# Layer norm as a multiply-add with a precomputed offset, the next chunk's attention norm begun three slots earlier, V projections with a nearer due time

## The chip, the cores and the metric

The kernel runs on one core of a Trainium2 chip. The metric is the device time of one execution in microseconds (us). Engine names follow the profile: PE is the matrix engine (PEld its weight loads), DVE the vector engine, ACT the scalar engine, POOL is GpSimd, and SP is the engine whose queue issues most DMAs here. DMAs are written SPq or POOLq by the queue that issues them. L12 is line 12 of the kernel before; the changed kernel's lines are numbered three higher between L176 and L474 (L182 before is L185 after, L215 is L218, L232 is L235, L339 is L342, L367 is L370).

## The reference, cut to what matters

Two identical layers, each a sliding-window attention (32 heads of 16, window 256) and a ReLU feed-forward (512 to 1792 to 512), each with a layer norm ahead and a residual behind. The sequence is 2048 tokens of width 512.

```python
def _layernorm(x, axis=-1, eps=1e-5):
    m = jnp.mean(x, axis=axis, keepdims=True)
    v = jnp.var(x, axis=axis, keepdims=True)
    return (x - m) / jnp.sqrt(v + eps)
...
    x = x + _A_ref(_layernorm(x, axis=-1), A_wqkv, A_wo)   # qkv, masked softmax, wo
    x = x + _B_ref(_layernorm(x, axis=-1), B_w1, B_w2)     # relu(x @ w1) @ w2
    x = x + _A_ref(_layernorm(x, axis=-1), A_wqkv, A_wo)
    x = x + _B_ref(_layernorm(x, axis=-1), B_w1, B_w2)
```

## The kernel before, in words

The sequence is cut into chunks of 512 tokens, four per layer, so there are eight **steps** k = 0 to 7 (layer k // 4, chunk k mod 4). Every step has 20 **slots**: four head groups t (u counts them through the program) times five groups g of key blocks. Slot 47, say, is step 2, slot +7. All activations stay in SBUF: x_sb holds the residual rows in fp32.

In one slot the program emits, in this order on PE: the score matmuls into Sps (S below), half of the slot's dense budget, the matmuls of probabilities and V into acc (A below, for the head group of five slots ago), and the other half of the budget. Beside them ACT computes the exponentials (Pb<-Sps, L251, two per slot), and the masks are set by DVE (L271) for groups 0, 3 and 4 and by POOL (L257, affine select, six per slot) for groups 1 and 2. The whole order of the matmuls is fixed: in_order (L85) ties each to the one before. The order on the other engines is chosen by the tile scheduler.

The dense budget (L524 to L543) is about nine 512-column matmuls per slot, taken by run_tasks (L447) from a list of tasks with an earliest slot and a due slot; the ready task with the nearest due slot goes first, and equal ones in the order in which they were added. The tasks are: Q and K projections of head group t (add_qk, 8 matmuls, due at slot 20k + 5t - 2), V projections of 128 tokens (add_v, 4 matmuls each), the output projection of half a chunk (plan_wo, 8 matmuls, O below, due at once), and the feed-forward of a chunk (plan_ffn, 56 + 56 matmuls, due late: 20(k+1) + 32). force (L458) runs overdue tasks at once, but only those whose due slot is 3 modulo 5. All dense matmuls share two PSUM buffers, ps_d, which DVE empties (L199, L215, L232, L339, L354, L367).

The layer norm (ln_rows, L178) of a chunk takes, for each 128 tokens, the statistics on DVE (L171, L172, L174), the power -1/2 on POOL (L175, result rstd), the subtraction and multiplication on POOL (L182, result xnA for attention or xnB for the feed-forward, two buffers each), and a transposing DMA from SP's queue into xnT or xn2T (L184). xnT and xn2T have one buffer each. So the transposes for the next chunk wait until the last Q, K or V matmul of the present chunk has read xnT. Tokens 2 and 3 of four (in blocks of 128) wait on POOL besides, until blocks 0 and 1 have been transposed out of the two xnA buffers.

For step k + 1, begin (L491) emits this norm in slot 20k + 5, and its Q, K and V tasks may start from slot 20k + 8. The feed-forward norm of step k is emitted behind its two output projections, around slots +4 and +6 of the next step. The first chunk's norm is written out by itself (L470 to L480) with PE transposes instead of DMAs: L474 runs on DVE for even blocks and on POOL for odd ones.

Of the kernel before, what the change touches and what calls it, by code (L numbers as in the profile page):

```python
# [9 lines left out]
FP32 = mybir.dt.float32  # L10
# [39 lines left out]
def kernel(  # L50
# [10 lines left out]
    nc = tc.nc  # L61
    S = A_x.shape[1]
# [5 lines left out]
    KC = D // P  # L68
# [9 lines left out]
    small = ctx.enter_context(tc.tile_pool(name="small", bufs=2))  # L78
# [18 lines left out]
    def mmt(o, i, idn):  # L97
        inst = nc.tensor.transpose(o, i, idn)
        if chained[0]:
            in_order(inst)  # L100
# [66 lines left out]
    def ln_stats(c, sfx, j0, j1, src=None):  # L167
        mv = small.tile([P, 4, 2], FP32, name="mv" + sfx)
        for j in range(j0, j1):
            st = small.tile([P, 6], FP32, name="st" + sfx)  # L170
            nc.vector.bn_stats(out=st[:], in_=x_sb[:, 4 * c + j, :] if src is None else src[:, j, :])  # L171
            nc.vector.bn_aggr(out=mv[:, j, :], in_=st[:])  # L172
        rstd = small.tile([P, 4], FP32, name="rstd" + sfx)
        nc.vector.tensor_scalar_add(rstd[:, j0:j1], mv[:, j0:j1, 1], 1e-5)  # L174
        nc.gpsimd.tensor_tensor(out=rstd[:, j0:j1], in0=rstd[:, j0:j1], in1=mhalf[:, j0:j1], op=ALU.pow)  # L175
        return rstd, mv  # L176

    def ln_rows(c, xnT, sfx, j0, j1):  # L178
        rstd, mv = ln_stats(c, sfx, j0, j1)
        for j in range(j0, j1):  # L180
            xn = work.tile([P, D], BF16, name="xn" + sfx, bufs=2)
            nc.gpsimd.tensor_scalar(out=xn[:], in0=x_sb[:, 4 * c + j, :], scalar1=mv[:, j, 0:1],  # L182
                                    scalar2=rstd[:, j:j + 1], op0=ALU.subtract, op1=ALU.mult)
            nc.sync.dma_start_transpose(out=xnT[:, :, j * P:(j + 1) * P],  # L184
                                        in_=xn[:].rearrange("p (kc d) -> p kc d", kc=KC))  # L185

# [4 lines left out]
    def q_items(xnT, Qt, t):  # L191
        ps = []

        def one(kc):
            if kc == 0:
                ps.append(ps_d.tile([P, 512], FP32, name="ps_d"))
            mm(ps[0][:], wqkv[:, kc, t * P:(t + 1) * P], xnT[:, kc, :], kc == 0, kc == KC - 1)
            if kc == KC - 1:
                nc.vector.tensor_copy(Qt[:], ps[0][:])  # L199
        return [lambda kc=kc: one(kc) for kc in range(KC)]  # L200

    def k_items(layer, c, xnT, t):
        ps = []
        s0 = slot(layer, 8 * c)
        runs = [(0, 8)] if s0 + 8 <= NSLOT else [(0, NSLOT - s0), (NSLOT - s0, 8)]

        def one(kc):
            if kc == 0:
                ps.append(ps_d.tile([P, 512], FP32, name="ps_d"))
            mm(ps[0][:], wqkv[:, kc, D + t * P:D + (t + 1) * P], xnT[:, kc, :], kc == 0, kc == KC - 1)  # L210
            if kc == KC - 1:
                for a, b in runs:
                    sa = (s0 + a) % NSLOT
                    for e in range(2):
                        nc.vector.tensor_scalar(out=KBD[:, t, sa:sa + b - a, 64 * e:64 * e + 64],  # L215
                                                in0=ps[0][:, 64 * a:64 * b].rearrange("p (s k) -> p s k", k=64),
                                                scalar1=par[:, e:e + 1], scalar2=None, op0=ALU.mult)
        return [lambda kc=kc: one(kc) for kc in range(KC)]  # L218
# [155 lines left out]
    SPS = 20  # L374
# [13 lines left out]
    def start_qkv(k):  # L388
        xnTs[k] = work.tile([P, KC, 512], BF16, name="xnT", tag="xnT", bufs=1)

    def add_qk(k, t, earliest):
        layer, c = divmod(k, NCH)
        holder = {}

        def make():
            Q[k, t] = work.tile([P, 512], BF16, name="Qt", bufs=6)
            return q_items(xnTs[k], Q[k, t], t) + k_items(layer, c, xnTs[k], t)

        def first():
# [68 lines left out]

    start_qkv(0)
    for h in range(2):  # L470
        rstd0, mv0 = ln_stats(0, "S%d" % h, 2 * h, 2 * h + 2, src=xst0)
        for j in range(2 * h, 2 * h + 2):
            xn = work.tile([P, D], BF16, name="xnA", bufs=2)
            (nc.gpsimd if j % 2 else nc.vector).tensor_scalar(  # L474
                out=xn[:], in0=xst0[:, j, :], scalar1=mv0[:, j, 0:1], scalar2=rstd0[:, j:j + 1],
                op0=ALU.subtract, op1=ALU.mult)
# [3 lines left out]
            (nc.scalar.copy if j % 2 else nc.vector.tensor_copy)(xnTs[0][:, :, j * P:(j + 1) * P], tp[:])  # L480
# [19 lines left out]
    def total_left():  # L500
        return sum(len(x[3]) for x in tasks)
# [169 lines left out]
```

## Time and profile before

| what | value |
|---|---|
| time, median of 2 runs | 679.56 us (679.39 to 679.73) |
| profiled execution, own time | 677.07 us |
| its span, first to last instruction | 675.3 us |
| PE busy in the span | 501.4 us (74%) |
| DVE, POOL, ACT busy | 392.9, 326.8, 295.2 us |
| mean granted PE clock | 0.878 |
| PE waiting for xnT | 71.8 us in 6 waits |

The span is 1.8 us shorter than the same execution's time, which has the launch and the end around it. A row of the timeline gives a start, a length, the engine, the line, output and inputs, a count where instructions are merged, and in square brackets how long the engine had stood idle and what ended that. A busy PE is not PE at its peak, so the idle rows and the granted clock tell more than the 74%.

### The profile page before, as it was taken

The page shows a single profiled execution, that of the slowest core. Times are in us where ns is not written, and L with a number is a line of the kernel's source. Part 1 is how long each engine was busy: PE and PEld are TensorE (multiplying, and loading weights), DVE is VectorE, ACT ScalarE, POOL GpSimd, SP SyncE. Part 2 cuts the span into 40 slices and gives each one's busy share as a digit, 9 for nine tenths or more (in the row PEclk, how much of TensorE's full clock was granted, in tenths as well). Part 3 has the DMA queues.
Part 4 walks back from the last instruction along what each step waited for, and adds up shares of the span by engine and source line. Part 5 has one row for each costly group of instructions (what it writes and reads, how often), then busy time and mean ns, then how long its engine had stood idle before and what let it go on. Part 6 is the DMA issues. An engine that isn't in the chain of part 4 may idle for free.

```text
span 675.3 us, 13941 instructions
## 1 busy us (share of the span) xinstructions
PE 501.4 (74%) x5741; PEld 235.2 (35%) x5741; DVE 392.9 (58%) x914; ACT 295.2 (44%) x323; POOL 326.8 (48%) x505
## 2 busy tenths in 40 slices
PE   5658668899189980899648984589937996798194
PEld 2223333444034440344313441234413443344042
DVE  6868447867367580775728673385628647454161
ACT  1353765566235660465414562256534666262000
POOL 9854757224923459233582255523575346332501
PEclk8879659999779995899969996799979999798698
DMA  9410111002200022001210012000230012003102
GB/s 295 172 32 1 34 32 33 2 1 33 55 9 2 2 48 47 1 2 10 54 34 1 2 24 55 16 3 9 49 55 17 2 33 48 17 9 56 32 1 37
DMA packets 59001, 23.02 MB, mean 34 GB/s; under 512 B 50480, under 2 KB 58416, under 8 KB 58928
## 3 DMA queue, kind: packets, MB, share of 16 engines
q1 hardware_dynamic: 56624, 19.94, 13.2%
q0 software_dynamic: 2304, 2.10, 2.1%
q8 instruction: 47, 0.77, 0.5%
q14 instruction: 26, 0.21, 0.1%
HBM read 7.86 MB, written 2.10 MB: 15 GB/s over the span
## 4 chain that ended last, share of the span: by engine, by line
PE 40%; DVE 22%; POOL 18%; issue 11%; DMA 5%; ACT 3%; SPq 0%; POOLq 0%; ACTq 0%
PE ps_d L93 30%; DVE V L232 8%; POOL xnB L182 7%; PE acc L93 6%; PE Sps L93 4%; DVE KBD L215 4%; POOL xnA L182 4%; POOL Pb L257 3%; DVE Pb L271 3%; ACT Pb L251 3%; DMA xnT<-xnA 3%; DMA OT<-O 2%; POOL rstdB L175 1%; DVE stB L171 1%; DVE x_sb L339 1%
## 5 line engine op out<-in xcount | busy, mean ns | idle before, releaser
L251 ACT ACTIVATE Pb<-Sps 128x1024 bf16<-128x1024 f32 (+2 forms) x320 | 292.7, 968 | 301.4 <-PE Sps L93 186.4
L257 POOL TENSOR_SCALAR_AFFINE_SELECT Pb<-Pb 64x256 bf16<-64x256 bf16 x368 | 153.3, 417 | 208.7 <-ACT Pb L251 190.3
L93 PE MATMUL ps_d<-xnT,wqkv 128*128 128x512 bf16 x256 | 79.5, 434 | 82.8 <-DMA xnT<-xnA 71.8
L93 PE MATMUL ps_d<-xn2T,w 128*128 128x512 bf16 x448 | 117.9, 387 | 26.2 <-DMA xn2T<-xnB 21.3
L93 PE MATMUL ps_d<-w,hT 128*128 128x512 bf16 x448 | 112.5, 379 | 0.0
L93 PEld LDWEIGHTS <-Pb 128*128 128x128 bf16 x2880 | 95.8, 97 | 44.7 <-issue 11.7
L354 DVE TENSOR_SCALAR hT<-ps_d 128x512 bf16<-128x512 f32 x112 | 76.3, 687 | 54.5 <-PE ps_d L93 54.4
L93 PE MATMUL acc<-V,Pb 128*128 128x34 bf16 x2880 | 98.6, 179 | 2.4 <-POOL Pb L257 2.1
L93 PE MATMUL Sps<-Qt,KBD 32*128 32x320 bf16 (+4 forms) x1408 | 71.4, 267 | 18.5 <-ACT Pb L251 16.8
L271 DVE TENSOR_TENSOR Pb<-Pb,tri 128x512 bf16<-128x512 bf16 (+1 forms) x152 | 60.1, 425 | 35.4 <-ACT Pb L251 34.6
L182 POOL TENSOR_SCALAR xnB<-x_sb,mvB,rstdB 128x512 bf16<-128x512 f32 x32 | 67.0, 2097 | 1.8 <-DMA xn2T<-xnB 0.2
L199 DVE CAST Qt<-ps_d 128x512 bf16<-128x512 f32 x32 | 22.0, 687 | 75.2 <-PE ps_d L93 75.0
L93 PEld LDWEIGHTS <-wqkv 128*128 128x128 bf16 x256 | 22.9, 106 | 117.8 <-issue 87.5
L93 PEld LDWEIGHTS <-w 128*128 128x128 bf16 x448 | 37.2, 98 | 72.0 <-issue 38.3
L182 POOL TENSOR_SCALAR xnA<-x_sb,mvA,rstdA 128x512 bf16<-128x512 f32 x28 | 57.8, 2071 | 8.4 <-DMA xnT<-xnA 7.7
L232 DVE CAST V<-ps_d 64x256 bf16<-64x256 f32 x128 | 54.0, 422 | 2.1
L93 PEld LDWEIGHTS <-KBD 32*128 32x128 bf16 x1408 | 25.7, 93 | 83.4 <-issue 79.7
L215 DVE TENSOR_SCALAR KBD<-ps_d,par 128x512 bf16<-128x512 f32 (+1 forms) x80 | 47.2, 634 | 11.6 <-PE ps_d L93 11.6
L93 PEld LDWEIGHTS <-hT 128*128 128x128 bf16 x448 | 37.4, 97 | 41.6 <-issue 6.9
L93 PE MATMUL ps_d<-wo,OT 128*128 128x512 bf16 x128 | 38.8, 434 | 13.0 <-DMA OT<-O 9.3
L93 PE MATMUL ps_d<-wqkv,xnT 128*128 128x512 bf16 x128 | 37.8, 382 | 13.4 <-DVE V L232 6.6
L367 DVE TENSOR_TENSOR x_sb<-ps_d,x_sb 128x512 f32<-128x512 f32 x32 | 22.0, 689 | 36.9 <-PE ps_d L93 34.9
(59 smaller groups left out, 228.9 us busy)
## 6 DMA issues: line engine op xcount, KB each, us to landing
w<-in_B_w_dram SPq DMA_DIRECT2D x2, 1792.0 KB, 13.7
out_dram<-x_sb POOLq DMA_DIRECT2D x16, 128.0 KB, 2.8
wqkv<-in_A_wqkv_dram SPq DMA_DIRECT2D x3, 512.0 KB, 6.6
xst<-in_A_x_dram SPq DMA_DIRECT2D x3, 512.0 KB, 9.3
xst<-in_A_x_dram SPq DMA_DIRECT2D x2, 256.0 KB, 3.2
wo<-in_A_wo_dram SPq DMA_DIRECT2D x1, 512.0 KB, 8.8
OT<-O SPq DMA_TRANSPOSE x32, 2.5
xn2T<-xnB SPq DMA_TRANSPOSE x32, 2.4
```

The costliest lines, as they stand in the source:

```text
L93: inst = nc.tensor.matmul(o, lhsT=lhsT, rhs=rhs, start=start, stop=stop)
L171: nc.vector.bn_stats(out=st[:], in_=x_sb[:, 4 * c + j, :] if src is None else src[:, j, :])
L175: nc.gpsimd.tensor_tensor(out=rstd[:, j0:j1], in0=rstd[:, j0:j1], in1=mhalf[:, j0:j1], op=ALU.pow)
L182: nc.gpsimd.tensor_scalar(out=xn[:], in0=x_sb[:, 4 * c + j, :], scalar1=mv[:, j, 0:1], scalar2=rstd[:, j:j + 1], op0=ALU.subtract, op1=ALU ...
L199: nc.vector.tensor_copy(Qt[:], ps[0][:])
L215: nc.vector.tensor_scalar(out=KBD[:, t, sa:sa + b - a, 64 * e:64 * e + 64], in0=ps[0][:, 64 * a:64 * b].rearrange("p (s k) -> p s k", k=64 ...
L232: nc.vector.tensor_copy(V2[64 * e:64 * e + 64, sl, :, 17 * e:17 * e + 16], v4[64 * half:64 * half + 64, :, e, :])
L251: nc.scalar.activation(pv4[:, 2 * rp:2 * rp + 2, 64 + a:64 + z], Sps[rp][:, :, a:z], ACT.Exp, scale=0.25)
L257: nc.gpsimd.affine_select(out=v, in_=v, pattern=[[0, 4], [-1 if far else 1, 64]], compare_op=ALU.is_gt if far else ALU.is_ge, fill=0.0, ba ...
L271: nc.vector.tensor_tensor(out=v, in0=v, in1=m, op=ALU.min)
L354: nc.vector.tensor_relu(hT[:, f, n0:n1], ps[0][:, n0:n1])
L367: nc.vector.tensor_tensor(out=x_sb[:, b, :], in0=ps[0][:], in1=x_sb[:, b, :], op=ALU.add)
```

## The change

Four edits. ln_stats computes one more small vector on DVE, nb = -mean times rstd, behind the power on POOL, and returns it instead of the means. ln_rows on POOL then does x times rstd plus nb instead of (x minus mean) times rstd. The first chunk's norm does the same as an ACT activation (Identity, with scale rstd and bias nb) for all four blocks. begin moves from slot 20k + 5 to 20k + 2, the earliest slot of the Q and K tasks from 20k + 8 to 20k + 5, that of the V tasks to 20k + 7, and the due slot of the V tasks from 20k + 3 to 20k - 1 (which is 4 modulo 5, so that force no longer takes them).

```diff
@@ ln_stats, ln_rows
-        return rstd, mv
+        nb = small.tile([P, 4], FP32, name="nb" + sfx)
+        nc.vector.scalar_tensor_tensor(out=nb[:, j0:j1], in0=mv[:, j0:j1, 0], scalar=-1.0, in1=rstd[:, j0:j1],
+                                       op0=ALU.mult, op1=ALU.mult)
+        return rstd, nb
...
-            nc.gpsimd.tensor_scalar(out=xn[:], in0=x_sb[:, 4 * c + j, :], scalar1=mv[:, j, 0:1],
-                                    scalar2=rstd[:, j:j + 1], op0=ALU.subtract, op1=ALU.mult)
+            nc.gpsimd.tensor_scalar(out=xn[:], in0=x_sb[:, 4 * c + j, :], scalar1=rstd[:, j:j + 1],
+                                    scalar2=nb[:, j:j + 1], op0=ALU.mult, op1=ALU.add)
@@ add_v
-        add_task(earliest, SPS * k + 3, [first] + [lambda: holder["i"].pop(0)() for _ in range(KC - 1)])
+        add_task(earliest, SPS * k - 1, [first] + [lambda: holder["i"].pop(0)() for _ in range(KC - 1)])
@@ first chunk
-            (nc.gpsimd if j % 2 else nc.vector).tensor_scalar(
-                out=xn[:], in0=xst0[:, j, :], scalar1=mv0[:, j, 0:1], scalar2=rstd0[:, j:j + 1],
-                op0=ALU.subtract, op1=ALU.mult)
+            nc.scalar.activation(xn[:], xst0[:, j, :], ACT.Identity, bias=nb0[:, j:j + 1], scale=rstd0[:, j:j + 1])
@@ the steps
-        at_slot(SPS * k + 5, begin)
+        at_slot(SPS * k + 2, begin)
...
-            add_qk(k + 1, t, SPS * k + 8)
+            add_qk(k + 1, t, SPS * k + 5)
...
-            add_v(k + 1, j, SPS * k + 8)
+            add_v(k + 1, j, SPS * k + 7)
```

On PE the change moves the dense matmuls between slots. Step 2, counted from the two programs (Q for a Q or K projection, F1 and F2 for the feed-forward, bold for the chunk after):

| slot | before | after |
|---|---|---|
| 42 | S8 F2x4 A19 F2x5 | S8 F2x4 A19 F2x2 Qx3 |
| 43 | S12 F2x4 A19 F2x5 | S12 Qx4 A19 Qx1 |
| 44 | S12 Ox4 A19 Ox4 F2x1 | S12 Ox4 A19 Ox4 |
| 45 | S8 F2x5 A20 F2x2 Qx3 | S8 **Qx5** A20 **Qx5** |
| 46 | S8 Ox4 A19 Ox4 Qx1 | S8 Ox4 A19 Ox4 **Qx1** |
| 47 | S8 Qx4 A19 | S8 **Vx4** A19 **Vx5** |
| 48 | S12 **Qx4** A19 **Qx5** | S12 **Vx4** A19 **Vx3 Qx2** |
| 49 | S12 **Qx4** A19 **Qx3 Vx2** | S12 **Qx4** A19 **Qx5** |
| 50 | S8 **Vx4** A20 **Vx5** | S8 **Qx2** F1x2 A20 F1x5 |
| 51, 52 | **Vx5 Qx8** F1x5 | F1x18 |

The last matmul that reads the present chunk's xnT, and the first that needs the next one's, are neighbours before (slots 47 and 48), and have slot 44 between them after (slots 43 and 45). Steps 3, 4 and 6 read alike, with the last reader just ahead of the A run of slot +3 in steps 4 and 6. In step 5 it stands in slot +4, ahead of the A run there. In step 0 the change puts the first Q of chunk 1 directly behind chunk 0's last, in slots 4 and 5; before, slots 5 to 7 lay between.

POOL's queue in step 2 (rstdA and xnA belong to the attention norm, xnB and rstdB to the feed-forward's, Pb_132 is slots 46 and 47), before:

```order
L175 TENSOR_TENSOR rstdB<-rstdB,mhalf 128x2
L182 TENSOR_SCALAR xnB<-x_sb,mvB,rstdB 128x512 x2
L175 TENSOR_TENSOR rstdA<-rstdA,mhalf 128x4
L257 AFFINE_SELECT Pb_132<-Pb_132 64x4x64 x6
L175 TENSOR_TENSOR rstdB<-rstdB,mhalf 128x2
L257 AFFINE_SELECT Pb_132<-Pb_132 64x4x64
L182 TENSOR_SCALAR xnB<-x_sb,mvB,rstdB 128x512 x2
L257 AFFINE_SELECT Pb_132<-Pb_132 64x4x64 x2
L182 TENSOR_SCALAR xnA<-x_sb,mvA,rstdA 128x512 x2
L257 AFFINE_SELECT Pb_132<-Pb_132 64x4x64 x3
L182 TENSOR_SCALAR xnA<-x_sb,mvA,rstdA 128x512 x2
```

and in the changed kernel:

```order
L175 TENSOR_TENSOR rstdA<-rstdA,mhalf 128x4
L185 TENSOR_SCALAR xnA<-x_sb,rstdA,nbA 128x512 x4
L175 TENSOR_TENSOR rstdB<-rstdB,mhalf 128x2
L185 TENSOR_SCALAR xnB<-x_sb,rstdB,nbB 128x512 x2
L260 AFFINE_SELECT Pb_132<-Pb_132 64x4x64 x6
L175 TENSOR_TENSOR rstdB<-rstdB,mhalf 128x2
L185 TENSOR_SCALAR xnB<-x_sb,rstdB,nbB 128x512 x2
L260 AFFINE_SELECT Pb_132<-Pb_132 64x4x64 x6
```

The four xnA rows (blocks 2 and 3 of the next chunk, then blocks 0 and 1 of the one behind it) have moved from behind both feed-forward norms to ahead of both.

DVE's queue of the changed kernel in the same place, from the cast behind the first Q matmuls of slot 45 (KBD, V and Qt empty ps_d, L342 is the residual add of the output projection in slot 46):

```order
L174 TENSOR_SCALAR rstdB<-mvB 128x2
L202 CAST Qt<-ps_d 128x512
L177 SCALAR_TENSOR_TENSOR nbB<-mvB,rstdB 128x2
L218 TENSOR_SCALAR KBD<-ps_d,par 128x8x64 x2
L342 TENSOR_TENSOR x_sb<-ps_d,x_sb 128x512
L171 BN_STATS stB<-x_sb 128x6
L172 BN_AGGR mvB<-stB 128x2
L342 TENSOR_TENSOR x_sb<-ps_d,x_sb 128x512
L171 BN_STATS stB<-x_sb 128x6
L172 BN_AGGR mvB<-stB 128x2
L174 TENSOR_SCALAR rstdB<-mvB 128x2
L177 SCALAR_TENSOR_TENSOR nbB<-mvB,rstdB 128x2
```

Each nbB is new and stands in DVE's queue behind a power that POOL computes; the four V casts of slot 47 follow directly.

More of the change, by code (lines that the diff above doesn't have):

```diff
@@ L175, in ln_stats @@
         nc.gpsimd.tensor_tensor(out=rstd[:, j0:j1], in0=rstd[:, j0:j1], in1=mhalf[:, j0:j1], op=ALU.pow)
-        return rstd, mv
+        nb = small.tile([P, 4], FP32, name="nb" + sfx)
+        nc.vector.scalar_tensor_tensor(out=nb[:, j0:j1], in0=mv[:, j0:j1, 0], scalar=-1.0, in1=rstd[:, j0:j1],
+                                       op0=ALU.mult, op1=ALU.mult)
+        return rstd, nb
     def ln_rows(c, xnT, sfx, j0, j1):
-        rstd, mv = ln_stats(c, sfx, j0, j1)
+        rstd, nb = ln_stats(c, sfx, j0, j1)
         for j in range(j0, j1):
             xn = work.tile([P, D], BF16, name="xn" + sfx, bufs=2)
-            nc.gpsimd.tensor_scalar(out=xn[:], in0=x_sb[:, 4 * c + j, :], scalar1=mv[:, j, 0:1],
-                                    scalar2=rstd[:, j:j + 1], op0=ALU.subtract, op1=ALU.mult)
+            nc.gpsimd.tensor_scalar(out=xn[:], in0=x_sb[:, 4 * c + j, :], scalar1=rstd[:, j:j + 1],
+                                    scalar2=nb[:, j:j + 1], op0=ALU.mult, op1=ALU.add)
             nc.sync.dma_start_transpose(out=xnT[:, :, j * P:(j + 1) * P],
@@ L470 @@
     for h in range(2):
-        rstd0, mv0 = ln_stats(0, "S%d" % h, 2 * h, 2 * h + 2, src=xst0)
+        rstd0, nb0 = ln_stats(0, "S%d" % h, 2 * h, 2 * h + 2, src=xst0)
         for j in range(2 * h, 2 * h + 2):
             xn = work.tile([P, D], BF16, name="xnA", bufs=2)
-            (nc.gpsimd if j % 2 else nc.vector).tensor_scalar(
-                out=xn[:], in0=xst0[:, j, :], scalar1=mv0[:, j, 0:1], scalar2=rstd0[:, j:j + 1],
-                op0=ALU.subtract, op1=ALU.mult)
+            nc.scalar.activation(xn[:], xst0[:, j, :], ACT.Identity, bias=nb0[:, j:j + 1], scale=rstd0[:, j:j + 1])
             tp = ps_d.tile([P, KC, P], BF16, name="tp", tag="ps_d")
```

## The prediction

> **What bounds the kernel now.** I read the totals first, then PE's waits in order of size, then the timeline around each long one.
>
> ```profile
> span 675.3 us, 13941 instructions
> PE ps_d L93 <- DMA xnT<-xnA: 71.8, 6, 17.3
> PE ps_d L93 <- DMA xn2T<-xnB: 21.3, 2, 14.7
> PE ps_d L93 <- DMA OT<-O: 9.3, 4, 4.9
> ```
>
> The columns are total us, times, longest. PE follows a fixed order, so a matmul that waits holds everything behind it. The six waits for xnT, the normalised and transposed input of the next chunk, are the largest loss. They are these rows (the wait stands in brackets), with one wait for OT in the same step as the fifth:
>
> ```profile
> 49.96 1.87 PE L93 MATMUL ps_d<-xnT,wqkv 128*128 128x512 bf16 x4 [4.64 <-DMA xnT<-xnA]
> 187.07 1.87 PE L93 MATMUL ps_d<-xnT,wqkv 128*128 128x512 bf16 x4 [15.18 <-DMA xnT<-xnA]
> 269.13 1.87 PE L93 MATMUL ps_d<-xnT,wqkv 128*128 128x512 bf16 x4 [17.25 <-DMA xnT<-xnA]
> 346.57 1.86 PE L93 MATMUL ps_d<-xnT,wqkv 128*128 128x512 bf16 x4 [12.99 <-DMA xnT<-xnA]
> 408.79 1.89 PE L93 MATMUL ps_d<-wo,OT 128*128 128x512 bf16 x4 [4.91 <-DMA OT<-O]
> 429.16 1.87 PE L93 MATMUL ps_d<-xnT,wqkv 128*128 128x512 bf16 x4 [12.36 <-DMA xnT<-xnA]
> 503.32 1.87 PE L93 MATMUL ps_d<-xnT,wqkv 128*128 128x512 bf16 x4 [9.39 <-DMA xnT<-xnA]
> ```
>
> Together 76.7 us, one row or pair for each of steps 0 and 2 to 6. Why 15 us in step 2:
>
> ```profile
> 169.63 1.02 PE L93 MATMUL ps_d<-xnT,wqkv 128*128 128x512 bf16 x4 [0.24 <-DVE x_sb L339]
> 171.51 2.57 SPq L184 DMA_TRANSPOSE xnT<-xnA  x2
> 175.29 4.13 POOL L182 TENSOR_SCALAR xnB<-x_sb,mvB,rstdB 128x512 bf16<-128x512 f32 x2
> 180.38 4.12 POOL L182 TENSOR_SCALAR xnA<-x_sb,mvA,rstdA 128x512 bf16<-128x512 f32 x2
> 182.47 3.25 SPq L184 DMA_TRANSPOSE xnT<-xnA  x2
> ```
>
> The last reader of the old xnT ends at 170.65. Only then do the first two transposes go out, and only behind them can POOL write blocks 2 and 3, since xnA has two buffers. But POOL takes xnB first, so 16.4 us pass from the last reader to the next Q matmul, and PE has one run of work to put in between. The wait is a serial chain behind the release of xnT, not lack of POOL time as such.
>
> **The chain without POOL's detour.** Step 0 has it nearly bare:
>
> ```profile
> 38.88 1.04 PE L93 MATMUL ps_d<-xnT,wqkv 128*128 128x512 bf16 x4 [0.82 <-DVE KBD L215]
> L184 SPq DMA_TRANSPOSE xnT<-xnA x4: 1189/1190/1312, 40.1 to 47.4; - x4
> DMA to landing us min/median/max: 2.4/2.5/3.1
> 42.87 2.08 POOL xnA L182
> 47.41 2.41 DMA xnT<-xnA
> ```
>
> Released at 39.92, issued at 40.1 (0.2), landed after 2.5, two POOL rows of 2.07, the last transpose 2.4, and 0.15 to the matmul: 9.4 us (10.0 measured there, with a power in between).
>
> **Term 1, the waits: -35.3 us.** In the changed POOL queue the xnA rows stand ahead of xnB, so I take 9.4 for the chain. Between release and first use now lies slot 44's work, whose size is seen before:
>
> ```profile
> 158.61 0.40 PE L93 MATMUL Sps<-Qt,KBD 32*128 32x64 bf16 x12
> 158.94 1.04 PE L93 MATMUL ps_d<-wo,OT 128*128 128x512 bf16 x4
> 159.82 0.63 PE L93 MATMUL acc<-V,Pb 128*128 128x34 bf16 x19
> 161.62 0.38 PE L93 MATMUL ps_d<-w,hT 128*128 128x512 bf16 x1
> 161.93 0.40 PE L93 MATMUL Sps<-Qt,KBD 32*128 32x256 bf16 x8
> ```
>
> A slot start to the next is 3.32; less one feed-forward matmul (0.38), plus the next S (0.40) and 0.3 for ACT's pace: 3.6 us of cover. Steps 2 and 3 then wait 9.4 - 3.6 = 5.8 each. Steps 4 and 6 have an A run more (0.6): 5.2 each. In step 5 the release stands in slot +4, with 0.9 of cover, and one xnB row precedes xnA on POOL (1.8 more): 10.3. In step 0 nothing but an S lies between (0.3): 9.1, worse than its 4.64 now. Sum 41.4 against 76.7. The transposes for OT's second half now queue on SP behind xnT's four; they go out when the last xnT one does, and their matmuls come a slot after the first Q, so they are covered. The wait never falls below 5 us, so PE's cold restart stays: four matmuls in 1.87 instead of 1.04.
>
> **Term 2, the start: -2.5 us.**
>
> ```profile
> 9.93 2.08 POOL L474 TENSOR_SCALAR xnA<-xst,mvS,rstdS 128x512 bf16<-128x512 bf16 x1
> 11.69 0.11 DVE L155 MEMSET V<- 64x64 bf16 x1 [0.26 <-issue]
> 13.85 0.59 ACT L480 COPY xnT<-tp 128x512 bf16<-128x512 bf16 x1 [11.79 <-PE tp L98]
> 16.53 2.10 POOL L474 TENSOR_SCALAR xnA<-xst,mvS,rstdS 128x512 bf16<-128x512 bf16 x1
> 19.96 3.06 PE L93 MATMUL ps_d<-xnT,wqkv 128*128 128x512 bf16 x8 [0.67 <-ACT xnT L480]
> ```
>
> nbS stands in DVE's queue behind ten memsets, the last at 11.69, so ACT begins at 12.0. Four activations and two copies at 0.6 to 0.7 each, with the PE transposes between, end near 16.7 instead of 19.9: 3 us, of which I give back 0.5, since nbA of chunk 1 makes DVE wait for POOL's casts ahead of the first Qt. The Trainium skill (ScalarE: Activation LUTs, What ACT_TABLE_LOAD costs) has an activation with two pointer operands at about 0.8 us for this size, an estimate from its formula, against 0.59 for the copy row; that would take 0.5 us more from this term.
>
> **Term 3, moved slots: -2.5 us.** Three slots with nothing but S and A leave the stretch of steps 0 and 1 that goes at ACT's pace:
>
> ```profile
> 70.40:107.80 37.40, 25.34 (x363) 13.15 (x361) 16.66 (x45) 25.23 (x29) 25.42 (x36) 0.59 0.18 36
> L251 ACT ACTIVATE Pb<-Sps 128x1024 bf16<-128x1024 f32 x272 | 263.6, 1021 | 268.1 <-PE Sps L93 153.2 <-issue 89.6 <-ACT Pb L251 23.2
> ```
>
> That is 14.5 slots in 37.4 us with 16 cold O matmuls in it: 2.4 us a slot, near two exponentials of 1.02. The three are done later at PE's own 1.2 a slot, which saves 3.6; step 7 gets two such slots more than before (its Q work is done earlier) and pays about 1.1 net.
>
> **Term 4, new holds: +12 us.** This is what the change adds. nb on DVE waits for rstd from POOL, and POOL is deep in xnA and xnB by then.
>
> ```profile
> L182 POOL TENSOR_SCALAR xnB<-x_sb,mvB,rstdB 128x512 bf16<-128x512 f32 x32 | 67.0, 2097 | 1.8 <-DMA xn2T<-xnB 0.2 <-POOL rstdB L175 0.2
> L175 POOL TENSOR_TENSOR rstdB<-rstdB,mhalf 128x2 f32<-128x2 f32 x16 | 11.7, 729 | 60.0 <-DVE rstdB L174 59.7
> L257 POOL TENSOR_SCALAR_AFFINE_SELECT Pb<-Pb 64x256 bf16<-64x256 bf16 x368 | 153.3, 417 | 208.7 <-ACT Pb L251 190.3
> ```
>
> With R the release: POOL's xnA rows end at R + 12 (the last two wait for a landing). The first nbB stands behind a Qt cast that itself comes at R + 11.7 and so costs half a microsecond. POOL's first xnB pair ends at R + 17 (power 0.7, pair 4.2), six affine selects (2.5, and they wait for slot 46's exponentials) near R + 20, the second power at R + 21; DVE reaches its nbB near R + 19.7 and is held 1.3, with V casts behind it and PE behind those. The projection stretch also gets O's two adds and statistics, which DVE used to do before the wait. How much that costs is seen from two stretches with the same 40 projection matmuls:
>
> ```profile
> 187.07:205.30 18.23, 16.15 (x172) 6.92 (x173) 13.29 (x29) 7.43 (x8) 5.55 (x8) 0.84 0.01 1
> 107.80:124.60 16.80, 13.73 (x176) 6.24 (x173) 14.69 (x35) 9.38 (x10) 9.70 (x15) 1.00 0.09 18
> ```
>
> The first follows a wait (clock 0.84), the second has the statistics in it (DVE x35) and no wait ahead, and is no longer. So 1.5 us per step for the holds, 9 in six steps. xn2T is next: its second half is ready about 13 us after slot 46's O, by then PE has done some 13 us of projections and wants it in slot 50, two slots sooner than now. I give 0.5 a step, 3 in all; without this cover a step would lose up to 4.
>
> **Term 5, POOL's multiply-add: 0.** No row shows it. The nearest:
>
> ```profile
> L182 POOL TENSOR_SCALAR xnA<-x_sb,mvA,rstdA 128x512 bf16<-128x512 f32 x28 | 57.8, 2071 | 8.4 <-DMA xnT<-xnA 7.7
> L484 POOL CAST x_sb<-xst 128x512 f32<-128x512 bf16 x12 | 6.8, 608 | 0.0
> ```
>
> Same operand shapes, two operations, two pointers: I take 2.07. From below it could be a cast's 0.61, from above the sum of the two, 2.68. Two of these rows lie in each of six chains, two in step 7's wait for xn2T (21.3 less 14.7: 6.6) and some two in the tail's 14.7: sixteen rows on the path, so -23 us to +10 us. The Trainium skill (GPSIMD Engine Reference, 3.1 Elementwise) puts a one-input body at 1.03 to 1.8 cycles an element; that is 0.44 to 0.77 us here, an estimate, and by it the sum would be some 20 to 26 us lower. The subtract-multiply row, at 2.07, does not agree with it.
>
> **Sum.** -35.3 - 2.5 - 2.5 + 12 = -28.3. Against the profiled execution's own 677.07 that is 648.8. The median of the runs shown lies 2.5 above that execution, so I forecast **651 us**.
>
> **Rivals.** (a) *Multiply-add is cheap on POOL.* For it: 2.07 us is 3.4 casts, which looks like a general loop; against it: nothing in the trace has another price for two operations. At 1.0 us a row, 16 rows give -17: **634 us**. (b) *The wait moves to xn2T.* For it: slot 50 wants xn2T two slots sooner, and POOL's norm for it now starts 12 us after the release. Against it: the projections are mostly DVE's time and slow enough. At 3 us in each of six steps in place of 0.5: **666 us**. (c) *Slower: DVE held by POOL's power.* One in-order queue holds casts for PE behind nb, and nb behind POOL's backlog of xnB, affine selects and power (4.2 + 2.5 + 0.7 = 7.4 us). If DVE stands through all of it at the second nbB, and 2.3 us at each of the other two, that is about 12 us a step in six steps, 72 in place of 9 + 3: 60 more, **711 us**; over 6 to 7 us a step it is slower than before. Against it: the scheduler puts work ahead of each nb, and PE itself is late there. (d) *It does not start sooner:* the last Q of the present chunk still decides the release, and if the chain from there is 15 us as now (POOL held elsewhere), only the cover counts: 3.6 in five steps, and step 0 loses 5; with terms 2 to 4 that is about **676 us**.
>
> **Chances.** Forecast 0.55, (a) 0.22, (b) 0.10, (c) 0.07, (d) 0.06. About 2% is what a measurement can tell from no change, so faster means below 666. Nearly all of the forecast's share and (a), and half of (b), fall there: 0.80. Within 2%: half of (b), (d) and a little of the forecast, 0.13. Slower: 0.07. The range must take in most of (a) and (b): 628 to 672.
>
> **What would show it.** Waits for xnT of 5 to 6 us in steps 2, 3, 4 and 6, about 10 in 0 and 5, some 41 in all; POOL's L185 rows at 2.07; first Q near 17 us; waits for xn2T hardly above 21 in all; DVE waiting for POOL's rstd in each step, for 1 to 2 us. Wrong would be: waits for xnT much under 30 or over 60, new waits of PE for xn2T or for POOL's masks above 10 us in all, or DVE held for 5 us at a time.

## The result, and the profile after

| | before | changed kernel |
|---|---|---|
| median of the runs shown | 679.56 us | 652.67 us (651.83 to 653.51, 2 runs) |
| profiled execution, own time | 677.07 us | 651.83 us |
| span | 675.3 us | 650.1 us |
| POOL busy | 326.8 us | 243.6 us |
| DVE busy | 392.9 us | 397.5 us |
| mean granted PE clock | 0.878 | 0.876 |

The ratio of the times is 0.960 (95% interval 0.955 to 0.966). The forecast was 651 us. That it came so near is partly luck, as the rest of this document shows: a term put at 0 was worth -22.4 us, and a loss of 18.4 us that no term has stood against it.

PE's waits in the changed kernel (total us, times, longest), to be set beside the rows of before in the prediction:

```profile
PE ps_d L93 <- DVE V L235: 36.8, 30, 2.6
PE ps_d L93 <- DMA xnT<-xnA: 22.2, 5, 7.6
...
PE ps_d L93 <- DMA xn2T<-xnB: 13.5, 2, 11.1
...
PE ps_d L93 <- DMA OT<-O: 5.4, 3, 3.3
```

The waits for xnT have gone from 71.8 to 22.2 us, which is 50 us and not the 35 of the forecast (that one with a wait for OT in it). The largest loss is now another one: PE waits 36.8 us for the casts that empty a V projection out of ps_d. Before, the profile's row for the same wait was this:

```profile
PE ps_d L93 <- DVE V L232: 13.5, 32, 0.8
```

The number of waits is about the same, but the longest is 2.6 us instead of 0.8. The waits for xnT that are left stand in these rows of PE's timeline:

```profile
47.15 1.87 PE L93 MATMUL ps_d<-xnT,wqkv 128*128 128x512 bf16 x4 [7.34 <-DMA xnT<-xnA]
...
254.44 1.24 PE L93 MATMUL ps_d<-xnT,wqkv 128*128 128x512 bf16 x5 [0.41 <-DMA xnT<-xnA]
...
322.89 2.31 PE L93 MATMUL ps_d<-xnT,wqkv 128*128 128x512 bf16 x5 [4.54 <-DMA xnT<-xnA]
...
396.82 2.29 PE L93 MATMUL ps_d<-xnT,wqkv 128*128 128x512 bf16 x5 [7.56 <-DMA xnT<-xnA]
...
467.45 1.74 PE L93 MATMUL ps_d<-xnT,wqkv 128*128 128x512 bf16 x6 [2.32 <-DMA xnT<-xnA]
```

They belong to steps 0, 3, 4, 5 and 6. In step 2, where 15.18 us were lost before, no wait for xnT is left. The main reason why they are shorter than forecast is seen in POOL's rows (count, then total us and ns of one):

```profile
L185 POOL TENSOR_SCALAR xnB<-x_sb,rstdB,nbB 128x512 bf16<-128x512 f32 x32 | 24.3, 769 | 7.7 <-DVE nbB L177 5.4 <-DMA xn2T<-xnB 1.7 <-DVE mvB L172 0.3
L185 POOL TENSOR_SCALAR xnA<-x_sb,rstdA,nbA 128x512 bf16<-128x512 f32 x28 | 23.0, 822 | 23.4 <-DMA xnT<-xnA 21.5 <-DVE Pb L274 1.4 <-DVE mvA L172 0.4
```

A row of the multiply-add takes 0.77 to 0.82 us, where the subtract-multiply took 2.07 to 2.10. The Trainium skill (GPSIMD Engine Reference, 3.1 Elementwise) gives 1.8 cycles an element as a best case, 0.77 us for 512 elements; for the multiply-add the trace agrees, for the subtract-multiply it does not.

**The new loss.** This is PE's timeline where the V projections of step 2 stand in slots 47 and 48 (a row with wqkv,xnT is a V projection, one with xnT,wqkv would be Q or K; in brackets the idle time before it):

```profile
187.21 1.02 PE L93 MATMUL ps_d<-wqkv,xnT 128*128 128x512 bf16 x4 [0.24 <-DVE x_sb L342]
188.07 0.63 PE L93 MATMUL acc<-V,Pb 128*128 128x34 bf16 x19
191.05 1.04 PE L93 MATMUL ps_d<-wqkv,xnT 128*128 128x512 bf16 x4 [2.34 <-DVE V L235]
193.91 0.61 PE L93 MATMUL ps_d<-wqkv,xnT 128*128 128x512 bf16 x1 [1.83 <-DVE V L235]
194.46 0.61 PE L93 MATMUL Sps<-Qt,KBD 32*128 32x320 bf16 x12
195.00 1.46 PE L93 MATMUL ps_d<-wqkv,xnT 128*128 128x512 bf16 x3
198.98 0.61 PE L93 MATMUL ps_d<-wqkv,xnT 128*128 128x512 bf16 x1 [2.52 <-DVE V L235]
```

And DVE's in the same stretch:

```profile
189.19 0.16 DVE L177 SCALAR_TENSOR_TENSOR nbB<-mvB,rstdB 128x2 f32<-128x2 f32 x1 [0.88 <-POOL rstdB L175]
189.26 1.73 DVE L235 CAST V<-ps_d 64x256 bf16<-64x256 f32 x4
...
192.13 1.73 DVE L235 CAST V<-ps_d 64x256 bf16<-64x256 f32 x4 [0.39 <-PE ps_d L93]
196.50 1.29 DVE L235 CAST V<-ps_d 64x256 bf16<-64x256 f32 x3 [2.64 <-PE ps_d L93]
```

PE and DVE take turns: the matmuls of 191.05 end at 192.09, their casts run from 192.13 to 193.86, the next matmul starts at 193.91, ends with its group at 196.46, and the next casts start at 196.50. With two ps_d buffers PE would fill one while DVE empties the other. So only one buffer seems to be in use here, which the experiments below test. The table of slots in the part on the change says where the other one is: in slots 45 and 46 PE does 5 + 5 + 1 = 11 projections of Q and K, which is two groups of four and three quarters of a third. Then the V tasks become ready (earliest 20k + 7) with a nearer due slot than the Q task has, so the third group stays open, with its buffer, until all sixteen V matmuls are done. PE's waits for V casts come to 8.1, 8.1 and 7.3 us in steps 1, 2 and 6, which show this pattern, and to 2.8 to 3.5 us each in steps 3 to 5.

### The profile page after: what moved, and what is told of

It is laid out like the page before. It is cut to its first block, busy times and chain, and to the rows that moved or that the text cites. A ratio compares the mean times of both kernels' runs of the same rounds, so it can differ in the third digit from the quotient of the medians.

```text
span 650.1 us, 13961 instructions
## 1 busy us (share of the span) xinstructions
PE 513.6 (79%) x5741; PEld 237.7 (37%) x5741; DVE 397.5 (61%) x937; ACT 298.5 (46%) x327; POOL 243.6 (37%) x503
## 5 line engine op out<-in xcount | busy, mean ns | idle before, releaser
L93 PE MATMUL ps_d<-xn2T,w 128*128 128x512 bf16 x448 | 119.0, 391 | 19.6 <-DMA xn2T<-xnB 13.5
L93 PE MATMUL ps_d<-xnT,wqkv 128*128 128x512 bf16 x256 | 82.7, 443 | 37.8 <-DMA xnT<-xnA 22.2
L93 PE MATMUL Sps<-Qt,KBD 32*128 32x320 bf16 (+4 forms) x1408 | 71.8, 271 | 18.1 <-ACT Pb L254 15.2
L274 DVE TENSOR_TENSOR Pb<-Pb,tri 128x512 bf16<-128x512 bf16 (+1 forms) x152 | 60.4, 427 | 38.0 <-ACT Pb L254 37.3
L93 PE MATMUL ps_d<-wqkv,xnT 128*128 128x512 bf16 x128 | 42.5, 448 | 29.9 <-DVE V L235 28.5
L218 DVE TENSOR_SCALAR KBD<-ps_d,par 128x512 bf16<-128x512 f32 (+1 forms) x80 | 47.7, 635 | 10.6 <-PE ps_d L93 10.5
L93 PE MATMUL ps_d<-wo,OT 128*128 128x512 bf16 x128 | 40.2, 450 | 15.6 <-DMA OT<-O 5.4
L93 PEld LDWEIGHTS <-hT 128*128 128x128 bf16 x448 | 36.9, 97 | 39.8 <-issue 6.8
L370 DVE TENSOR_TENSOR x_sb<-ps_d,x_sb 128x512 f32<-128x512 f32 x32 | 22.1, 690 | 29.7 <-PE ps_d L93 26.7
L283 DVE RECIPROCAL chk<-acc 128x16 f32<-128x16 f32 x64 | 16.2, 253 | 35.0 <-PE acc L93 34.8
L342 DVE TENSOR_TENSOR x_sb<-ps_d,x_sb 128x512 f32<-128x512 f32 x32 | 22.0, 686 | 21.9 <-PE ps_d L93 21.9
L185 POOL TENSOR_SCALAR xnA<-x_sb,rstdA,nbA 128x512 bf16<-128x512 f32 x28 | 23.0, 822 | 23.4 <-DMA xnT<-xnA 21.5
```

Source lines behind the costliest of these rows:

```text
L93: inst = nc.tensor.matmul(o, lhsT=lhsT, rhs=rhs, start=start, stop=stop)
L274: nc.vector.tensor_tensor(out=v, in0=v, in1=m, op=ALU.min)
L283: nc.vector.reciprocal(rinv, acc[:, :, :, 16:17])
L342: nc.vector.tensor_tensor(out=x_sb[:, qb, :], in0=ps[0][:], in1=x_sb[:, qb, :], op=ALU.add)
L370: nc.vector.tensor_tensor(out=x_sb[:, b, :], in0=ps[0][:], in1=x_sb[:, b, :], op=ALU.add)
```

## The experiments

Times are medians. In brackets stand the ratio to the kernel before, which was measured beside each, and its 95% interval. The kernel before ran at 680.8 us beside the first four, at 678.7 beside the next four, at 680.6 beside the next three and at 680.2 beside the last. The deadline of a task is its due slot.

**The multiply-add alone** (before, with ln_stats and ln_rows of the change):

```diff
-            nc.gpsimd.tensor_scalar(out=xn[:], in0=x_sb[:, 4 * c + j, :], scalar1=mv[:, j, 0:1],
-                                    scalar2=rstd[:, j:j + 1], op0=ALU.subtract, op1=ALU.mult)
+            nc.gpsimd.tensor_scalar(out=xn[:], in0=x_sb[:, 4 * c + j, :], scalar1=rstd[:, j:j + 1],
+                                    scalar2=nb[:, j:j + 1], op0=ALU.mult, op1=ALU.add)
```

> The kernel before with the multiply-add on POOL alone (slots, due times and the first chunk's norm as before). Theory A, POOL's price: the changed kernel's rows take 0.77 us instead of 2.07, and the kernel before has four of them (two xnB, two xnA) in the chain behind each release. Each of the five long waits falls by 5.2, step 0's by 2.6, step 7's and the tail's waits for xn2T by 2.6 and 3.6: about -35 us, 645 us. Theory B, the earlier begin is what gained: the multiply-add alone leaves most of the waits, 665 us or more. A third possibility, DVE held by the power behind nb, would show as waits of DVE for POOL above 30 us in all.

Measured: **643.9 us** (0.946, 0.941 to 0.951). This one edit gains 36.9 us and beats the whole change by 9.

```profile
PE ps_d L93 <- DMA xnT<-xnA: 41.0, 6, 8.9
...
PE ps_d L93 <- DVE V L235: 14.8, 30, 0.9
```

The waits for xnT fall from 71.8 to 41.0 with the norm still begun at 20k + 5, and the waits for V casts stay near where they were before (14.8 against 13.5). DVE waits 27.7 us for rstd here, a little under the 30 of the third possibility, and the time is still close to the 645 that the price of the row gives.

**The change without the multiply-add** (the changed kernel with the old rows; nb is not computed for them, so nothing holds DVE either):

```diff
-            nc.gpsimd.tensor_scalar(out=xn[:], in0=x_sb[:, 4 * c + j, :], scalar1=rstd[:, j:j + 1],
-                                    scalar2=nb[:, j:j + 1], op0=ALU.mult, op1=ALU.add)
+            nc.gpsimd.tensor_scalar(out=xn[:], in0=x_sb[:, 4 * c + j, :], scalar1=mv[:, j, 0:1],
+                                    scalar2=rstd[:, j:j + 1], op0=ALU.subtract, op1=ALU.mult)
```

> The changed kernel with the subtraction and multiplication back on POOL (begin, due times and the ACT norm of the first chunk stay). It is what the prediction's sum was made for. Theory A: sixteen rows on the path at 1.3 us more each, 673 us (668 to 680), waits for xnT near 41 us. Theory B: the earlier begin covers the rows, 660 us or less.

Measured: **668.5 us** (0.983, 0.978 to 0.989), a gain of 12.3, just inside the 668 to 680 of theory A.

```profile
PE ps_d L93 <- DMA xnT<-xnA: 47.7, 6, 12.4
PE ps_d L93 <- DVE V L232: 33.8, 31, 2.8
PE ps_d L93 <- DMA xn2T<-xnB: 20.6, 2, 14.7
```

With rows of 2.08 us the waits for xnT are 47.7, near the forecast's 41.4. But the waits for V casts are already there, without any nb: the new loss comes from neither the row nor the hold.

**V's due slot back** (the changed kernel, one number):

```diff
-        add_task(earliest, SPS * k - 1, [first] + [lambda: holder["i"].pop(0)() for _ in range(KC - 1)])
+        add_task(earliest, SPS * k + 3, [first] + [lambda: holder["i"].pop(0)() for _ in range(KC - 1)])
```

> The changed kernel with the V tasks due at 20k + 3 again, so that the begun Q group is finished before the V groups start. Theory H, a held buffer: in steps 1, 2 and 6 a Q group is left open with one of the two ps_d buffers while four V groups go through the other, each PE group waiting for the casts of the one before; closing it takes the waits for the V casts from 36.8 us back to about 14 to 18, 632 us (628 to 640). Rival D: DVE's sixteen casts of 0.42 us per chunk set the pace whatever the order; then 650 us, within 3.

Measured: **634.3 us** (0.932, 0.927 to 0.937). The nearer deadline costs the change 18.4 us.

```profile
PE ps_d L93 <- DMA xnT<-xnA: 25.0, 5, 7.8
PE ps_d L93 <- DVE V L235: 20.9, 27, 2.4
```

The waits for V casts fall by 16 us: no group stands open when V's turn comes, since the first two Q and K tasks now go first. (This profile is of the slowest execution, 639.1 us, and 95 of 5741 matmul records are missing from it, so its waits may be a little off.) The windows show what may be a second part of the price. Of the changed kernel and of this one, 15 us each among step 2's projections (busy us per engine, then the granted clock):

```profile
190.00:205.00 15.00, 8.21 (x71) 2.99 (x72) 8.34 (x21) 2.90 (x4) 3.40 (x8) 0.66 0.09 19
```

```profile
185.00:200.00 15.00, 10.02 (x126) 4.45 (x128) 13.58 (x31) 5.92 (x7) 4.15 (x9) 1.00 0.12 20
```

With the buffer held, DVE is busy 8.3 of 15 us instead of 13.6, and the granted clock is 0.66 instead of 1.00, though no gap there is longer than 2.52 us.

**A begun group is finished first** (the changed kernel; the deadline stays, run_tasks takes no other task while a Q, K or V group of four is open):

```diff
             x = min(ready, key=lambda y: (y[1], y[2]))
+            if cur[0] is not None and len(cur[0][3]) % 4 != 0 and len(cur[0][3]) < 8:
+                x = cur[0]
             x[3].pop(0)()
+            cur[0] = x
```

> The changed kernel with its due times, but a Q, K or V group of four matmuls is finished once it is begun, ahead of any other task (a rule in run_tasks). Theory H: the held buffer is gone for the V groups and also for the output projection of slot +6; 630 us (625 to 638), waits for V casts 14 to 18 us in steps 1, 2 and 6 like those of steps 3 to 5. Rival D: no change, 650 us within 3.

Measured: **635.4 us** (0.934, 0.929 to 0.939). Closing the group gives back 17.3 of the 18.4 us with the deadline left as it is, so it is the open group that costs, and the deadline mainly through it. The rule does a little more than that: it also closes the Q group that stands open while the output projection of slot 46 runs, and what this part is worth here was not measured apart. The waits for V casts fell less far than they should have by this theory, to 25.0 (21 waits, the longest 3.9). The longest in step 2 is this row of PE, with this row of DVE just ahead of it:

```profile
186.53 1.77 PE L93 MATMUL ps_d<-wqkv,xnT 128*128 128x512 bf16 x4 [3.94 <-DVE V L235]
```

```profile
185.41 0.16 DVE L177 SCALAR_TENSOR_TENSOR nbB<-mvB,rstdB 128x2 f32<-128x2 f32 x1 [2.33 <-POOL rstdB L175]
```

DVE stands 2.33 us at nbB for POOL's power, with the next V casts behind it. Steps 1 and 6 show the like (waits of PE of 3.94 and 3.61 us behind holds of DVE of 2.04 and 2.20). So with the buffer free, these three waits come largely from the hold.

**The norm begun at 20k + 5 again** (the changed kernel; multiply-add and V's nearer deadline kept):

```diff
-        at_slot(SPS * k + 2, begin)
+        at_slot(SPS * k + 5, begin)
...
-            add_qk(k + 1, t, SPS * k + 5)
+            add_qk(k + 1, t, SPS * k + 8)
...
-            add_v(k + 1, j, SPS * k + 7)
+            add_v(k + 1, j, SPS * k + 8)
```

> The changed kernel with begin at slot 20k + 5 and Q, K and V from 20k + 8 again (multiply-add, ACT norm and the nearer V due slot stay). With equal earliest slots a Q group is never left open for the V groups, so the held buffer goes with the early begin. Theory now: the early begin by itself is worth about 7 us where POOL's rows are cheap, and costs about 18 us by the held buffer. So this kernel comes to 641 us (637 to 645), with waits for xnT near 41 us and for the V casts near 15 us. Rival: the early begin is the larger part of the gain; then 660 us or more.

Measured: **645.3 us** (0.949, 0.945 to 0.953), 7 less than the changed kernel and just above the 637 to 645 expected. Here Q and V tasks become ready in the same slot, so that the eight matmuls of the nearest Q and K go first and no group is left open; the waits for V casts are 19.4. So in the change as it stands the earlier start is a loss: it opens, with the nearer deadline, the groups that cost 18.4 us, and gains only some 10. The gain is 9.6 from the multiply-add alone (643.9) to 634.3, with the first norm on ACT in it, and 11.0 from this kernel to 634.3, with the order of the V tasks in it.

**Which operation is dear on POOL** (a single run; xnA as add then multiply, xnB as multiply then subtract):

```diff
+                nc.gpsimd.tensor_scalar(out=xn[:], in0=x_sb[:, 4 * c + j, :], scalar1=nb[:, j:j + 1],
+                                        scalar2=rstd[:, j:j + 1], op0=ALU.add, op1=ALU.mult)
...
+                nc.gpsimd.tensor_scalar(out=xn[:], in0=x_sb[:, 4 * c + j, :], scalar1=rstd[:, j:j + 1],
+                                        scalar2=nb[:, j:j + 1], op0=ALU.mult, op1=ALU.subtract)
```

> A look at the price of POOL's row by form, in the changed kernel: xnA as add of -mean, then multiply by rstd; xnB as multiply by rstd, then subtract of mean times rstd (one small vector operation of DVE more per norm). If the order (multiply first) makes the row cheap, xnB reads 0.77 us and xnA 2.07; if the subtraction is what is dear, xnA 0.77 and xnB 2.07; if only multiply-then-add is cheap, both 2.07; if the input count or the shape decides, both 0.77.

Measured: 670.0 us, in that one run. Its two rows on POOL:

```profile
L193 POOL TENSOR_SCALAR xnB<-x_sb,rstdB,nbB 128x512 bf16<-128x512 f32 x32 | 66.6, 2088 | 10.9 <-issue 6.1 <-POOL rstdB L175 2.8 <-DVE chk_mn L324 0.6
L190 POOL TENSOR_SCALAR xnA<-x_sb,nbA,rstdA 128x512 bf16<-128x512 f32 x28 | 22.1, 792 | 22.4 <-DMA xnT<-xnA 19.1 <-DVE Pb L282 1.4 <-DVE chk_b L326 1.1
```

Add then multiply costs 0.79 us, multiply then subtract 2.09. Of the four forms priced in these runs the two with a subtraction are dear, in either order of the operations. Why a subtraction is dear is not shown.

**The first chunk's norm on DVE and POOL again** (the changed kernel, the fourth edit undone):

```diff
-            nc.scalar.activation(xn[:], xst0[:, j, :], ACT.Identity, bias=nb0[:, j:j + 1], scale=rstd0[:, j:j + 1])
+            (nc.gpsimd if j % 2 else nc.vector).tensor_scalar(
+                out=xn[:], in0=xst0[:, j, :], scalar1=mv0[:, j, 0:1], scalar2=rstd0[:, j:j + 1],
+                op0=ALU.subtract, op1=ALU.mult)
```

> The changed kernel with the first chunk's norm on DVE and POOL as before, and nothing else undone. The prediction's second term: 2.5 us slower than the changed kernel, 655 us, the first Q matmul near 20 us instead of 17.0. Rival: the start is hidden by the wait for xnT in step 0, which ends with a chain that starts from the last Q matmul of chunk 0 anyway; then the shift passes on in full, 3 us. A change of less than 1 us would mean that the start is not on the path.

Measured: **654.1 us** (0.962, 0.958 to 0.966), 1.5 above the changed kernel, with intervals that overlap. The first Q matmul of the changed kernel, and of this one:

```profile
17.03 2.29 PE L93 MATMUL ps_d<-xnT,wqkv 128*128 128x512 bf16 x5 [0.67 <-ACT xnT L481]
```

```profile
19.96 2.29 PE L93 MATMUL ps_d<-xnT,wqkv 128*128 128x512 bf16 x5 [0.67 <-ACT xnT L485]
```

The start is 2.9 us earlier, as forecast; how much of that reaches the end lies inside the measurement.

**Half of the V casts on ACT** (due slot back, groups finished, odd heads' casts on ACT):

```diff
-                        nc.vector.tensor_copy(V2[64 * e:64 * e + 64, sl, :, 17 * e:17 * e + 16],
-                                              v4[64 * half:64 * half + 64, :, e, :])
+                        (nc.scalar.copy if e else nc.vector.tensor_copy)(
+                            V2[64 * e:64 * e + 64, sl, :, 17 * e:17 * e + 16], v4[64 * half:64 * half + 64, :, e, :])
```

> What the runs so far point to: the changed kernel with V due at 20k + 3, groups of Q, K and V finished once begun, and half of the V casts (the odd heads) on ACT instead of DVE. With the buffers free the projection stretch should be paced by DVE's casts: eight of 0.42 us fewer per chunk, about 2 us of the 3.4 on the path in each of seven chunks: 620 us (612 to 628). Rival: the wait for casts is then a latency from matmul to cast, not DVE's rate, or the casts on ACT hold the exponentials: 633 us or more.

Measured: **648.1 us** (0.954, 0.950 to 0.958): a miss, 13.8 above the kernel with V's due slot back (634.3) and 12.7 above the one with groups finished (635.4). The two together with all casts on DVE were not run. A cast takes 395 ns on ACT and 419 on DVE, but the two engines do not work side by side:

```profile
PE ps_d L93 <- ACT V L235: 29.5, 24, 3.6
...
PE ps_d L93 <- DVE KBD L218: 18.4, 17, 3.8
```

```profile
ACT V L235 <- DVE V L235: 35.1, 36, 2.9
```

ACT's casts wait 36 times, 35.1 us in all, for a DVE cast into V. What ties them together (parts of one tile, or the order that the scheduler chose) was not tried.

**No hold of DVE** (the row as (x - mean) times rstd, with the minus mean written before the power, so DVE waits for nothing from POOL), first in the changed kernel:

```diff
-        nc.vector.scalar_tensor_tensor(out=nb[:, j0:j1], in0=mv[:, j0:j1, 0], scalar=-1.0, in1=rstd[:, j0:j1],
-                                       op0=ALU.mult, op1=ALU.mult)
+            nc.vector.tensor_scalar(out=nb[:, j0:j1], in0=mv[:, j0:j1, 0], scalar1=-1.0, scalar2=None, op0=ALU.mult)
...
+            nc.gpsimd.tensor_scalar(out=xn[:], in0=x_sb[:, 4 * c + j, :], scalar1=nb[:, j:j + 1],
+                                    scalar2=rstd[:, j:j + 1], op0=ALU.add, op1=ALU.mult)
```

> The changed kernel with its row as (x - mean) times rstd, minus the mean written by VectorE without a wait for GpSimd's power, so that VectorE no longer waits for rstd (20.9 us of such waits in the changed kernel's profile, 21 waits). Theory P (term 4 of the prediction: these holds cost TensorE 1.5 us in each of six steps): about 9 us below the changed kernel's 652.7, so 644. Rival N (the holds lie beside other work, what costs is the held ps_d buffer): 651 to 654, with TensorE's waits for V casts still near 37 us.

Measured: **645.7 us** (0.949, 0.946 to 0.953). The waits of DVE for rstd, in the changed kernel

```profile
DVE nbA L177 <- POOL rstdA L175: 11.1, 7, 2.1
...
DVE nbB L177 <- POOL rstdB L175: 9.8, 14, 1.9
```

are gone, and with them 7.0 us of time. The waits for V casts stay large, 32.6, and those for xnT rise from 22.2 to 29.2. In the same form with **V's due slot back**:

> The same row form in the kernel with V's deadline put back to slot 20k+3 (634.3 us, VectorE's waits for rstd 18.9 us). Theory P: 9 us less, 625. Rival N: 632 to 636, since in that kernel the waits for V casts are 20.9 us without the holds having changed.

Measured: **627.3 us** (0.921, 0.917 to 0.924), again 7.1 us less than with the hold (634.3). PE's waits now:

```profile
PE ps_d L93 <- DMA xnT<-xnA: 28.6, 5, 8.9
PE ps_d L93 <- DVE V L238: 19.7, 27, 1.7
...
PE ps_d L93 <- DVE KBD L221: 13.2, 20, 1.4
...
PE ps_d L93 <- DVE x_sb L345: 2.7, 9, 0.4
```

Those for xnT are 3.6 us longer than with the hold: PE seems to arrive sooner and wait there instead, so that part of what the hold cost is given back. And **with begun groups finished besides**:

> That kernel with each begun group of four projection matmuls finished before another task is taken. If the held buffer is closed once V's deadline is back, the rule adds nothing: the same as the kernel with V's deadline back and the new row form, within 3 us. If groups are still left open there (V waits of 20.9 us against 13.5 in the kernel before), up to 7 us less than that kernel.

Measured: **621.8 us** (0.915, 0.912 to 0.918), the fastest of all, 5.4 below the one before it. That is the second of the two outcomes expected, but the waits for V casts have no part in it:

```profile
PE ps_d L93 <- DVE V L238: 20.9, 29, 2.0
...
PE ps_d L93 <- DVE KBD L221: 11.0, 16, 1.4
```

PE's waits for KBD casts are 2.2 us less, and those for the residual adds of the output projection (x_sb, 2.7 us in nine waits) are gone. Both would follow if, without the rule, a Q group held a buffer while the output projection runs. Together they are 4.9 us, but this was not tested apart, and the two profiled executions differ by 8.3 us.

**The earlier start by itself** (the changed kernel with the old rows, no hold, and V's due slot back):

```diff
-        add_task(earliest, SPS * k - 1, [first] + [lambda: holder["i"].pop(0)() for _ in range(KC - 1)])
+        add_task(earliest, SPS * k + 3, [first] + [lambda: holder["i"].pop(0)() for _ in range(KC - 1)])
```

(against the change without the multiply-add, above)

> The changed kernel with the old subtract-multiply rows (2.08 us each, no hold of VectorE for rstd) and with V's deadline put back to slot 20k+3: what is left of the change is the earlier start and ScalarE's first norm. The prediction's own terms for just this are -35.3 - 2.5 - 2.5 and 3 for xn2T, so 642. Theory S (the held ps_d buffer costs the same 18 us with dear rows as with cheap ones, and the waits for xnT stay at 47.7): 668.5 less 18, 650, with TensorE's waits for V casts near 15 to 20 us in place of 33.8. Rival D (with dear rows GpSimd sets the pace of the projections, so the deadline matters little): 660 to 668.

Measured: **649.6 us** (0.957, 0.951 to 0.963). The open groups cost 18.9 us with dear rows too (668.5 less 649.6), so theory S held. The waits for xnT, one row for each step that the prediction named (the rows of 161.34 and 375.87 are the last readers of the old xnT in steps 2 and 5, and the row of POOL stands ahead of xnA in step 5):

```profile
45.72 1.87 PE L93 MATMUL ps_d<-xnT,wqkv 128*128 128x512 bf16 x4 [9.37 <-DMA xnT<-xnA]
...
161.34 0.38 PE L93 MATMUL ps_d<-xnT,wqkv 128*128 128x512 bf16 x1
...
172.62 1.89 PE L93 MATMUL ps_d<-xnT,wqkv 128*128 128x512 bf16 x4 [7.02 <-DMA xnT<-xnA]
...
244.17 2.29 PE L93 MATMUL ps_d<-xnT,wqkv 128*128 128x512 bf16 x5 [5.71 <-DMA xnT<-xnA]
...
315.98 2.32 PE L93 MATMUL ps_d<-xnT,wqkv 128*128 128x512 bf16 x5 [6.54 <-DMA xnT<-xnA]
...
375.87 0.82 PE L93 MATMUL ps_d<-xnT,wqkv 128*128 128x512 bf16 x3
...
390.81 2.29 PE L93 MATMUL ps_d<-xnT,wqkv 128*128 128x512 bf16 x5 [12.41 <-DMA xnT<-xnA]
...
463.95 2.31 PE L93 MATMUL ps_d<-xnT,wqkv 128*128 128x512 bf16 x5 [6.36 <-DMA xnT<-xnA]
```

```profile
379.98 4.14 POOL L182 TENSOR_SCALAR xnB<-x_sb,mvB,rstdB 128x512 bf16<-128x512 f32 x2
```

## Why the prediction came out right, term by term

The time was right to 2 us. The sum behind it was not. Laid out by pairs of kernels that differ in one piece (not all pairs were measured side by side; the kernel before differed by up to 2 us between such measurements):

| piece | forecast | measured | from |
|---|---|---|---|
| earlier start, first norm on ACT, moved slots, with xn2T's 3 (terms 1 to 3, part of 4) | -37.3 | -30.5 | 680.15 to 649.64 |
| rows of 0.77 to 0.79 instead of 2.08 us, no hold (term 5) | 0 | -22.4 | 649.64 to 627.25 |
| DVE held for rstd (term 4) | +9 | +7.1 | 627.25 to 634.31 |
| ps_d buffer held by an open group | not seen | +18.4 | 634.31 to 652.67 |
| sum | -28.3 | -27.4 | whole change: -26.9 |

Had POOL's row been as dear as the prediction took it to be, the forecast would have been too low by 17 us or more: with the old rows the change came to 668.5 us, and that without the hold.

**Term 1, the waits for xnT: the mechanism was right.** With the old rows, PE waits 9.4, 7.0, 5.7, 6.5, 12.4 and 6.4 us, where the prediction had 9.1, 5.8, 5.8, 5.2, 10.3 and 5.2: 47.4 in all against 41.4. Step 5 was the worst, as said. Each figure but step 3's is a little low, because the chain was put too short. In step 2 of that run the last reader ends at 161.72 and the next Q starts at 172.62, which is 10.9 us where the prediction took 9.4, while the cover is 3.9 where it took 3.6. In step 5 POOL has two xnB rows ahead of xnA and not one: 14.1 us (376.69 to 390.81) where the prediction's 9.4 and 1.8 give 11.2. In the changed kernel the waits were 22.2, outside the band of 30 to 60 that the prediction gave itself, and fell below its 5 us in four steps, to nothing in step 2. The rows in the chain had become cheap, and PE came later, held with DVE: without the hold the waits are 29.2, and 28.6 with V's deadline back. PE's restart stays slow after the waits of 4.5 us and more, as the prediction said (four matmuls in 1.87 us, five in 2.3, where the stretch of V projections has four in 1.04), and less so after the one of 2.32 us (six in 1.74).

**Terms 2 and 3.** The first Q starts at 17.03, where 17 was said, although the activation takes 0.81 us and not 0.6 to 0.7; undoing the edit costs about 1.5 us of the 2.5, inside the measurement. The moved slots were not measured apart.

**Term 4, the holds: right in kind and near in size.** DVE waits for rstd in each step, 1.6 us at a time for the attention norm and 0.7 for the feed-forward's (2.1 at most), 20.9 us in all, and the time pays 7 of them (9 forecast). The waits for xn2T are two, 13.5 us in all, and no new one appeared.

**Term 5, the multiply-add: this step failed.** The prediction took 2.07 us from the nearest row, the subtract-multiply of the same shapes, and kept 0.61 and 2.68 as bounds. The row is 0.77 to 0.82 us, and the gain, 22.4, sits at the lower bound of -23. Operand shapes were the wrong thing to match rows by; in the four forms measured, what decides is whether there is a subtraction in it. Rival (a) had this mechanism. Its 634 us is what the change reaches once V's deadline is put back (634.3), in part by luck, since it took 1.0 us a row and terms 1 to 3 gave 6.8 us less than forecast.

**What was not on the list: the open group.** The prediction quoted the table's slots and read them for the release and the cover, but not for the buffers. 11 projections ahead of the V tasks leave a group open, and the nearer due slot of the V tasks is the edit that puts sixteen V matmuls ahead of its last one. Rivals (b) and (c) looked for slower cases in xn2T and in DVE's queue; the loss sat in the matmul order that was already counted. It is 18.4 us in the time, and PE waits 23 us longer for V casts than before. Without it the change would have been worth 46.5 us. One sum among the rivals does not come out, though nothing hangs on it: the terms of (d) give 673.6 us and not 676.

The two gains do not add either. The multiply-add alone gives 36.9 us and the earlier start (with the first norm on ACT) 30.5, but together (634.3, with V's deadline back) 46.5 against 67.4: both shorten the same wait, so the second one finds less of it left. Taken after the multiply-add, the earlier start is worth 9.6.

## What to carry to other kernels

Do not price an operation on POOL by its operand shapes alone, since the arithmetic in it can decide, and where the bounds of one unknown row are wider than the rest of the sum, treat that row as the forecast's main question. When a table of priorities is changed, count the accumulation groups that stand open at each switch and the buffers that they hold: a group of four left at three turns two buffers into one. Two edits against one wait should be sized one after the other, not side by side.

## What the runs showed of the hardware

A two-operation TENSOR_SCALAR on POOL from 128x512 fp32 to bf16 takes 0.77 to 0.85 us as multiply-add, 0.77 to 0.86 as add-multiply, 2.07 to 2.11 as subtract-multiply and 2.09 as multiply-subtract (means of the 28 or 32 rows of each kind in a run). So the same function of x costs about 2.6 times as much when the offset is subtracted instead of added as its negative.

The granted PE clock fell to 0.66 over 15 us in which no gap was longer than 2.52 us, but PE was busy only 8.2 us of them; in the kernel with V's due slot back, PE was busy 10.0 of 15 us, no gap was longer than 1.74 us, and the clock was 1.00. The Trainium skill (TensorE: Matmul & The Clock Gate, HAM oscillation — how this bites in real kernels) has as its rule no idle gaps above about 3.4 us; here the clock fell with shorter ones in a row. The next section of the same page of the Trainium skill (A second HAM failure mode: psum-queue depth-cycling) has short idles between groups of matmuls do this, and the trace agrees with that.
